# The left-over rows of a feature transform, stacked within SBUF into one operand a quarter

## The chip, the cores and the metric

The kernel runs on one core of one Trainium2 chip. The metric is the device time of one execution in microseconds. The kernel before took 689.68 us as the median of three runs (688.99 to 689.81).

## What is computed

The reference is a transformer layer with a spectral mixer ahead of a gated network, for 2048 tokens of 640 features in float32.

```python
def _A_ref(x, w_r, w_i):
    X = jnp.fft.rfft2(x, axes=(-2, -1)) * (w_r + 1j * w_i)
    return jnp.fft.irfft2(X, s=(S, D), axes=(-2, -1))
h = x + _A_ref(_layernorm(x), A_w_r, A_w_i)
n = _layernorm(h)
out = h + ((n @ w_gate) * (n @ w_up)) @ w_down        # F = 1728
```

The two-dimensional transform is made of matrix products with tables of cosines and sines: the tokens in two steps (16 residues times 128), and the features in one. A real transform of 640 features has 321 frequencies, and 322 columns are kept (NQ).

## The kernel before

All work is put in order by hand. The tokens lie as 16 tiles of 128 partitions. The stages follow one another on TensorE:

- **Front** (lines 144 to 369). Each tile is loaded, its moments are taken, even and odd parts of the features are folded, and `s1_mm` makes the first token step. The result is `s1` (four quarters of 128 feature rows, float32) and `rest`, the left-over rows: with 161 folded rows a quarter does not fit 128 partitions, so 33 + 31 + 2 x 32 rows lie together in one tile of 128 partitions. `rest_split` (line 271) splits them into a high and a low part, `s1r[:, 0]` and `s1r[:, 1]`, so that the fast float32r passes of TensorE keep the accuracy: high x high, high x low and low x high.
- **The group loop** (lines 499 to 537). There are 16 groups (NG) of two frequencies and their mirrors. `d_mm(g)` is the feature transform of a group: four float32 products for the quarters against `fmt`, and then six float32r products of 322 columns for the left-over rows against `frt`. `d_out(g)` copies the result to SBUF on ScalarE in four pieces. `s2_mm(g)` is the second token step, into the one buffer `u`. `filt(g)` multiplies by the complex filter on VectorE: three instructions that read `u` and one that adds. `is2_mm(g - 1)` is the first inverse step, and `is2_out(g - 1)` takes its result out: `high` and `end` on ScalarE, `low` on VectorE, then `main` on ScalarE.
- **The rest** (lines 551 on): the inverse feature step, the second layernorm, and the gated network over 14 chunks, written as Strassen products. `t34(0)` (line 703) makes one of the operands of those products, `t3`, once for each half of the tokens.

In one turn of the loop TensorE has in its order: `s2_mm(g)`, `d_mm(g + 2)`, `is2_mm(g - 1)`. All the loads of the loop are issued by one queue, SyncE's: `load_wm(g + 3)` (128 KB of matrices, `bits`, and 644 KB of filter, `wts`) and `load_wi(g + 2)` (128 KB, `bits`). Each has three buffers that are used in turn, so `wts` of group g + 3 waits until `filt(g)` has read its own. The queue works in order: what is behind a waiting issue waits too. Each issue also takes one of eight completion semaphores in turn, and waits until the transfer eight places ahead of it has landed.

Of the kernel before, what the change touches and what calls it, by code (L numbers as in the profile page):

```python
# [12 lines left out]
F32R = mybir.dt.float32r  # L13
AF = mybir.ActivationFunctionType
# [7 lines left out]
NC = 14  # L22
FW = (160, 193, 161, 161)
FOFF = (0, 160, 353, 514)
NR = 4
AHEAD = 5
FOLDS = {0: (1, 2), 1: (3,), 2: (4,), 7: (9,), 9: (11,)}
# [11 lines left out]
def f32(ap):  # L39
    return ap.bitcast(F32)  # L40
# [29 lines left out]
def tile_spectral_glu(ctx: ExitStack, tc: tile.TileContext, x, wf, wgu, wlast, wdown, wdlast,  # L70
# [53 lines left out]
    def home(tag, shape, name, dt=F32):  # L124
        return keep.tile(shape, dt, tag=tag, name=name)

    def cut(t, o, *shape):
        v = t[:, o:o + int(np.prod(shape))]
        names = [f"d{i}" for i in range(len(shape))]
        return v.rearrange(f"p ({' '.join(names)}) -> p {' '.join(names)}", **dict(zip(names[1:], shape[1:])))  # L130

    tab = home("stage", [P, 1448], "tab")
    fmt, imt, cit = cut(tab, 0, 675), cut(tab, 676, 4, 161), cut(tab, 1320, P)
    frt = home("dA", [P, 2, 2, NQ], "frt", F32R)
    s1 = home("big", [P, 4, NG, P], "s1")
    s1r = home("wA", [P, 2, NG, P], "s1r", F32R)
    rest = home("qr", [P, NG, P], "rest")
# [167 lines left out]
    odd(0, nc.gpsimd)  # L305
    for t in range(NT):
        if t == 1:
            nc.gpsimd.dma_start(frt, frem)
        if t >= 1:
            fs = even(t)  # L310
            if t + 1 < NT and t + 1 not in ASIDE:
                fs.insert(1, (0.4, lambda: odd(t + 1, nc.vector)))
            if t < AHEAD:
                fs.insert(1 + (t <= 2), (0.2, lambda: scale_c(t)))
            if t == 1:
                fs, (recip, w, *left) = fs[1:], dve[1][0]
                for f in (c1[4], fs[0][1], fs[1][1], recip, fs[2][1], w):
                    f()
                dve[2].insert(0, left)
            elif t == 2:  # L320
                (ww, r), = dve[2]
                for f in (fs[0][1], ww, tail[2].pop(), fs[1][1], r, fs[2][1], fs[3][1]):
                    f()
            else:
                weave(fs, dve[t], t in FOLDS)
            for f in tail[t]:
                f()
            if t < AHEAD - 1:
                s1_rest(t - 1)
                main = lambda: s1_main(t - 1, PS1[t - 1][0], 0, 4)  # L330
                for f in acts[t][:1] + post[t] + ([*acts[t][1:], main] if t < 2 else [main, *acts[t][1:]]):
                    f()
            else:
                s1_main(t - 1, PS1[t - 1][0], 0, 4)
                s1_rest(t - 1)
                for f in post[t]:
                    f()
                if t + 1 in SCALE_ON_ACT:
                    scale_c(t + 1)
                for f in acts[t]:  # L340
                    f()
        else:
            e0 = [f for _, f in even(0)]
            c0[0]()
            for f in (e0[0], c0[1], e0[1], c0[2], c0[3], e0[2], c0[4], *f1[:-1]):
                f()
        if t in FOLDS:
            nc.gpsimd.tensor_copy(small.tile([P, 1], F32, tag="hold", name="hold"), folded(t)[1][:, 383:384])
            for k in FOLDS[t]:
                odd(k, nc.gpsimd)  # L350
        if t >= 1:
            for f in stats[t]:
                f()
            if AHEAD <= t + 1 < NT and t + 1 not in SCALE_ON_ACT:
                scale_c(t + 1)
        else:
# [22 lines left out]
    def load_wi(g):  # L379
        WI[g] = wis[g % 3]  # L380
        nc.sync.dma_start(WI[g], mm[g, :, 1])
# [5 lines left out]
    def parts(ps, main, rest):  # L387
        for k, (b, o, w, l, r) in enumerate(main):
            mmx(ps[b][:, o:o + w], l, r, k < 2, False)
        for k, (b, l, r) in enumerate(rest):  # L390
            mmx(ps[b][:, 0:NQ], l, r, False, k >= len(rest) - 2)

    def d_mm(g):
        ps = PD[g] = bank("re"), bank("im")
        where = ((1, 0), (0, 0), (1, 160), (0, 160))
        main = [(b, o, FW[c], s1[:, c, g], fmt[:, FOFF[c]:FOFF[c] + FW[c]]) for c, (b, o) in enumerate(where)]
        parts(ps, main, [(b, s1r[:, k, g], frt[:, l, b]) for k, l in ((0, 0), (0, 1), (1, 0)) for b in range(2)])

    def d_out(g):
        ps = PD[g]  # L400
# [98 lines left out]
    for g in range(3):  # L499
        load_wm(g)  # L500
        load_wi(g)
    d_mm(0)
    d_out(0)
    d_mm(1)
    d_out(1)
    for g in range(NG - 1):
        s2_mm(g)
        if g + 2 < NG:
            d_mm(g + 2)
        if g + 3 == NG:  # L510
            xt = home("big", [P, 2, 5, 2, 512], "xt", F32R)
            irt = xt[:, 1].rearrange("p k l n -> p (k l n)")[:, 0:5 * NQ].rearrange("p (c q) -> p c q", c=5)
            nc.gpsimd.dma_start(irt, irem)
        if g == NG - 2:
            s2_mm(g + 1)
            filt_half(g, 0, True)
            is2_out(g - 2)
        if g >= 1:
            is2_mm(g - 1)
        if g < NG - 2:  # L520
            filt(g)
        else:
# [12 lines left out]
        if g == 6:  # L535
            nc.sync.dma_start(cit, ci)
            nc.sync.dma_start(imt, imain)
# [164 lines left out]

    def t34(m):
        src = TJ["b"][:, :, 2 * m:2 * m + 2].rearrange("p j k n -> p k j n")
        hi, lo = ((t3[:, :, l] if m == 0 else xt[:, 1, 0:2, l]).rearrange("p k (j n) -> p k j n", j=4)
                  for l in range(2))
        if m:
            return [lambda: act(hi, src, AF.Copy), lambda: tt(lo, src, f32(hi), op=OP.subtract)]

        def low():  # L710
            for k in range(2):
                nc.vector.scalar_tensor_tensor(lo[:, k], src[:, k], -1.0, f32(hi[:, k]), op0=OP.mult, op1=OP.subtract)

        return [lambda: act(hi, src, AF.Copy, scale=-1.0), low]

    def transp(t):
        turn_mm(t)
# [77 lines left out]
    for t in range(NT):  # L795
        for k in tside[t]:
            turn_mm(k)
        if t + 2 < NT:
            unfold(t + 2, dside[t], tside[t])
        else:  # L800
            for k in tside[t]:
                turn_hi(k)
                turn_lo(k)
        if t + 3 < NT:
            id_mm(t + 3)
        for f in aside[t]:
            f()
        if t == NT - 3:
            is1_mm(t)
            ht = home("qm", [P, 9216], "ht", F32R)  # L810
            hop, t3 = cut(ht, 0, 7, 2, 512), cut(ht, 7168, 2, 2, 512)
# [136 lines left out]
    def strassen(c, blk, ahead, downs, side):  # L948
# [46 lines left out]
        product(oa, False, ws, 640, [(t3[:, k, 0], t3[:, k, 1]) for k in range(2)])  # L995
        tt(c22, oa, c22, op=OP.add)
        tt(ob if odd else h1, ob, c22, op=OP.mult)  # L997
        if odd:
# [42 lines left out]
    for n, (blk, p) in enumerate(steps):  # L1041
        if p == 6:
# [28 lines left out]
            else:  # L1071
# [25 lines left out]
                    return pieces((t1s[:, 0, m, k], t1s[:, 1, m, k]), pb[k])  # L1097

                def t34(m, k):
                    return pieces((t3[:, k, 0], t3[:, k, 1]), pd[k], -1) if m == 0 else pieces(  # L1100
                        (xt[:, 1, k, 0], xt[:, 1, k, 1]), pb[k])

                hi(0, range(2))
# [148 lines left out]
def tables():  # L1252
# [19 lines left out]
    def rows(kind, ds):  # L1272
        r = np.zeros((len(ds), 2, NQ))
        for i, d in enumerate(ds):
# [3 lines left out]
            else:  # L1278
# [7 lines left out]
    frem = np.concatenate([rows("ee", np.arange(128, 161)), rows("oe", np.arange(1, 32)),  # L1286
                           np.stack([rows("os", np.arange(1, 33)), rows("eo", np.arange(32))], 1).reshape(64, 2, NQ)])

    m = np.zeros((32, 128, 128), np.float64)
    im = np.zeros((32, 128, 128), np.float64)  # L1290
    kidx = np.zeros((32, 64), np.int64)
# [46 lines left out]
    for b in range(2):  # L1338
# [1 line left out]
        irem[0:64, (2, 4)[b]] = rest[b, :, 1]  # L1340
    irem[0, 3] = irem[64, 3] = inv[0, 192, 0]

    return dict(cc=f4(fwd), ci=f4(fwd.T), fmain=f4(fmain), frem=split(frem), imain=f4(imain), irem=irem,
                mm=f4(mm)), fr, kidx


# [32 lines left out]
```

## Time and profile before

| What | Value |
|---|---|
| median of three runs | 689.68 us |
| the profiled execution's own time | 689.28 us |
| its span on the core | 687.5 us |
| TensorE busy in the span | 676.1 us (98%) |
| VectorE, ScalarE, GpSimd busy | 70%, 47%, 56% |
| group loop, first `s2_mm` to last | 42.63 to 106.40 us |
| granted TensorE clock | 1.0 in every slice |

The profile is of one execution, and 1.8 us of its time lie outside the span. The table's busy shares are means over stages with different limits. The group loop, which the change touches, is about a tenth of the span. Times in the views count from the span's start.

### The profile page before, as it was taken

What the parts mean: (1) busy time and instruction counts of PE and PEld (TensorE: products, weight loads), DVE (VectorE), ACT (ScalarE), POOL (GpSimd) and SP (SyncE); (2) the same over time, 40 slices, a digit from 0 to 9 for tenths busy, and PEclk for the clock granted to TensorE, in tenths of its full rate; (3) what the DMA queues carried; (4) which work ended last, traced back from release to release, by engine and by line L of the source; (5) the groups of instructions that cost most, each with busy time, mean ns of one, the idle gap of its engine ahead of it and who ended that gap; (6) DMA issues with size and microseconds to landing.
All of it is one profiled execution on the core that took longest, in us unless ns stands there. A gap on an engine that the chain in (4) does not pass through costs nothing.

```text
span 687.5 us, 10293 instructions
## 1 busy us (share of the span) xinstructions
PE 676.1 (98%) x3744; PEld 597.6 (87%) x3744; DVE 483.4 (70%) x985; ACT 322.3 (47%) x623; POOL 383.0 (56%) x364
## 2 busy tenths in 40 slices
PE   8999999999999999999999999999999999999998
PEld 8989998887788888888888889788888888888887
DVE  7968887897963968786776647753757575766654
ACT  6966665375543434262635236542525252525310
POOL 3101114331097987787887623286987878797610
PEclk9999999999999999999999999999999999999999
DMA  9516663000121212125243239301212120212003
GB/s 328 203 55 215 238 205 119 1 1 26 52 78 39 76 39 77 40 82 106 82 62 99 89 75 275 111 0 40 78 39 77 39 77 38 77 40 77 1 1 153
DMA packets 43602, 60.30 MB, mean 88 GB/s; under 512 B 23584, under 2 KB 28448, under 8 KB 43552
## 3 DMA queue, kind: packets, MB, share of 16 engines
q1 hardware_dynamic: 42832, 57.78, 26.0%
q0 software_dynamic: 288, 1.48, 0.6%
q8 instruction: 29, 0.48, 0.3%
q10 hardware_dynamic: 432, 0.39, 0.2%
q14 instruction: 21, 0.17, 0.1%
HBM read 51.78 MB, written 7.86 MB: 87 GB/s over the span
## 4 chain that ended last, share of the span: by engine, by line
PE 75%; DVE 11%; DMA 5%; ACT 4%; POOL 2%; issue 2%; SPq 1%; DVEq 0%; ACTq 0%
PE e L110 37%; PE d L110 22%; PE re L110 2%; PE im L110 2%; PE u L414 2%; DMA x<-in_x_dram 2%; PE im L456 2%; PE eo L110 2%; DMA raw<-in_wgu_dram 2%; PE im L242 1%; DMA z<-zfar 1%; POOL wst L837 1%; PE ir L456 1%; DVE ht L942 1%; PE y L110 1%
## 5 line engine op out<-in xcount | busy, mean ns | idle before, releaser
L110 PE MATMUL e<-xt,wst 128*128 128x512 f32 x864 | 213.4, 391 | 0.2 <-ACT c L986 0.2
L110 PEld LDWEIGHTS e<-xt,wst 128*128 128x128 f32 x864 | 159.8, 188 | 31.1 <-ACT c L986 0.4
L923 DVE TENSOR_TENSOR x<-d,x 128x320 f32<-128x320 f32 x280 | 123.4, 484 | 48.7 <-PE d L110 44.5
L110 PE MATMUL d<-wd,ht 128*128 128x320 f32 x832 | 143.0, 308 | 0.0
L110 PEld LDWEIGHTS d<-wd,ht 128*128 128x128 f32 x832 | 130.8, 188 | 7.3
L837 POOL TENSOR_TENSOR wst<-raw,wst 128x1024 fp32r<-128x1024 f32 x23 | 56.3, 2449 | 64.5 <-ACT wst L836 63.3
L110 PE MATMUL e<-t,wst 128*128 128x512 f32 x288 | 74.1, 392 | 0.6 <-ACT h L978 0.6
L110 PE MATMUL d<-wt,ht 128*128 128x320 f32 x360 | 69.6, 311 | 0.5 <-DVE x L923 0.5
L853 POOL TENSOR_TENSOR wst<-raw,wst 128x896 fp32r<-128x896 f32 (+1 forms) x46 | 65.0, 1437 | 6.8 <-ACT wst L848 6.8
L110 PEld LDWEIGHTS e<-t,wst 128*128 128x128 f32 x288 | 52.7, 188 | 10.8 <-ACT h L978 1.4
L110 PEld LDWEIGHTS d<-wt,ht 128*128 128x128 f32 x360 | 57.3, 188 | 3.5 <-issue 1.0
L993 DVE TENSOR_TENSOR e<-e,h 128x512 f32<-128x512 f32 x24 | 16.8, 700 | 45.0 <-PE e L110 35.6
L848 ACT ACTIVATE wst<-raw 128x896 fp32r<-128x896 f32 (+1 forms) x48 | 30.2, 676 | 35.9 <-POOL raw L842 35.1
L978 ACT ACTIVATE h<-e 128x512 f32<-128x512 f32 x24 | 14.3, 596 | 68.3 <-PE e L110 63.6
L939 ACT ACTIVATE ht<-e 128x512 fp32r<-128x512 f32 x44 | 26.3, 597 | 40.4 <-DVE e L997 17.5
L485 POOL CAST qr<-bits 1x128 fp32r<-1x128 f32 x15 | 4.2, 280 | 71.4 <-DVE qr L489 71.4
L110 PE MATMUL e<-xt,wdir 128*128 128x512 f32 x180 | 42.6, 394 | 0.9 <-DVE ht L792 0.9
L110 PEld LDWEIGHTS e<-xt,wdir 128*128 128x128 f32 x180 | 33.4, 188 | 9.0 <-DVE ht L792 1.2
L942 DVE TENSOR_TENSOR ht<-e,ht 128x512 fp32r<-128x512 f32 x54 | 37.0, 686 | 1.6 <-ACT ht L939 1.3
L898 DVE TENSOR_TENSOR x<-d,x 128x320 f32<-128x320 f32 x62 | 27.5, 485 | 14.2 <-PE d L110 14.0
L110 PE MATMUL e<-ht,wst 128*128 128x512 f32 x144 | 37.1, 392 | 0.0
L581 ACT ACTIVATE wd<-draw 128x320 fp32r<-128x320 f32 (+1 forms) x30 | 15.7, 558 | 42.6 <-POOL draw L590 42.3
(213 smaller groups left out, 1230.6 us busy)
## 6 DMA issues: line engine op xcount, KB each, us to landing
raw<-in_wgu_dram SPq DMA_DIRECT2D x24, 640.0 KB, 3.9
wts<-in_wf_dram SPq DMA_DIRECT2D x16, 644.0 KB, 3.9
draw<-in_wdown_dram SPq DMA_DIRECT2D x24, 320.0 KB, 4.3
x<-in_x_dram SPq DMA_DIRECT2D x15, 320.5 KB, 6.0
out_dram<-x SPq DMA_DIRECT2D x15, 320.0 KB, 3.2
bits<-in_mm_dram SPq DMA_DIRECT2D x32, 128.0 KB, 3.8
zfar<-zr SPq DMA_DIRECT2D x32, 80.0 KB, 2.3
raw<-in_wgu_dram SPq DMA_DIRECT2D x4, 320.0 KB, 4.1
```

Of the source, the lines that this page charges most:

```text
L110: nc.tensor.matmul(o, l, r, start=start, stop=stop, skip_group_check=True)
L456: nc.tensor.matmul(out, y[:, h, a:b], inv(g, h), start=n == 0, stop=n == len(ys) - 1)
L581: act(o[:, 0, a:a + n], src, AF.Copy)
L837: ptt(wa[:, 1], stage[:, 0:1024], f32(wa[:, 0]), op=OP.subtract)
L848: act(ws[:, 0, o:o + b - a], stage[:, a:b], AF.Copy)
L853: ptt(ws[:, 1, o:o + b - a], stage[:, a:b], f32(ws[:, 0, o:o + b - a]), op=OP.subtract)
L898: tt(xv, ps[b][:, 0:320], xv, op=OP.add)
L923: tt(xv, o, xv, op=OP.add)
L939: act(hop[:, a, 0], src, AF.Copy)
L942: engine.tensor_tensor(hop[:, a, 1], src, f32(hop[:, a, 0]), op=OP.subtract)
L978: act(h0, oa, AF.Copy)
L993: tt(ob, ob, h1, op=OP.add)
```

## The change

For groups 3 to 15 the six float32r products of `d_mm` become four, one for each quarter of the output columns. Before, every product had all 128 left-over rows against all 322 columns of one half of the output, though a quarter's rows meet only their own 160 to 194 columns. Now a quarter's rows are stacked three times, high, low and high, on 93, 99, 96 and 96 partitions, against a table with high, high and low rows. One product over the stack gives the same three terms. Groups 0 to 2 keep the six products (PLAIN).

The stacks are made by `stack(g, n)`: for n groups at a time it issues, on SyncE's queue, 12 transfers from SBUF to SBUF, three for each quarter, of 31, 33, 32 and 32 rows, each row n x 512 bytes. There are two buffers: `dC` for three groups and `qt` for two. The stacks for groups 3 to 5 and 6 to 7 are issued ahead of the loop, those for groups 8 to 10, 11 to 12 and 13 to 15 in turns 3, 5 and 8 of the loop, when the buffer's last reader is in TensorE's order.

Besides, the table `frt` grows from 1288 to 1966 columns (one load on GpSimd's queue in the front stage), and since `qt` takes 4 KB of each partition, the tile `ht` is shorter, and `t3` lies in two tiles. In `t34(0)` ScalarE writes it with two instructions of 512 columns in place of one of 1024.

```diff
+RROWS = ((33, 31, 1), (0, 33, 1), (64, 32, 2), (65, 32, 2))
+RW = (160, 194, 162, 162)
+PLAIN = 3
+AGAIN = {3: (8, 3), 5: (11, 2), 8: (13, 3)}
...
-    frt = home("dA", [P, 2, 2, NQ], "frt", F32R)
+    frall = home("dA", [P, 4 * NQ + sum(RW)], "frt", F32R)
+    frt = cut(frall, 0, 2, 2, NQ)
...
-        parts(ps, main, [(b, s1r[:, k, g], frt[:, l, b]) for k, l in ((0, 0), (0, 1), (1, 0)) for b in range(2)])
+        if g < PLAIN:
+            parts(ps, main, [(b, s1r[:, k, g], frt[:, l, b]) for k, l in ((0, 0), (0, 1), (1, 0)) for b in range(2)])
+            return
+        parts(ps, main, [])
+        for q, ((r, n, _), (b, o), w) in enumerate(zip(RROWS, RWHERE, RW)):
+            a = 4 * NQ + sum(RW[:q])
+            mmx(ps[b][:, o:o + w], ST[g][0:3 * n, q], frall[0:3 * n, a:a + w], False, q >= 2)
...
+    def stack(g, n):
+        o = home("dC" if n == 3 else "qt", [P, 4, n, P], "st", F32R)
+        for q, (r, m, s) in enumerate(RROWS):
+            for i, l in enumerate((0, 1, 0)):
+                nc.sync.dma_start(f32(o[i * m:i * m + m, q]),
+                                  f32(s1r[r:r + s * (m - 1) + 1:s, l, g:g + n]))
...
+    stack(3, 3)
+    stack(6, 2)
     d_mm(0)
...
         if g + 2 < NG:
             d_mm(g + 2)
+        if g in AGAIN:
+            stack(*AGAIN[g])
...
-        return [lambda: act(hi, src, AF.Copy, scale=-1.0), low]
+        def high():
+            for k in range(2):
+                act(his[k], src[:, k], AF.Copy, scale=-1.0)
```

TensorE's order in one group, before: `d_mm` has the four products with `tab` and six with `frt` and `s1r`, and the inverse step (`ir`, `im` from `y`) follows.

```order
L110 MATMUL re<-tab,s_88 128x161
L110 MATMUL re<-frt,s1r 128x322
L110 MATMUL im<-frt,s1r 128x322
L110 MATMUL re<-frt,s1r 128x322
L110 MATMUL im<-frt,s1r 128x322
L110 MATMUL re<-frt,s1r 128x322
L110 MATMUL im<-frt,s1r 128x322
L456 MATMUL ir_705<-bits,y 65x32x4 x2
```

The same place now; `st` is the stack.

```order
L115 MATMUL re<-tab,s_88 128x161
L115 MATMUL im<-frt,st 128x160
L115 MATMUL re<-frt,st 128x194
L115 MATMUL im<-frt,st 128x162
L115 MATMUL re<-frt,st 128x162
L479 MATMUL ir_781<-bits,y 65x32x4 x2
```

Six rows of 322 columns became four of 160 to 194, and the half `re`, which ScalarE reads first, is now finished by the last row and not by the last but one.

SyncE's queue from the last load ahead of the loop (`bits` of the inverse matrices of group 2), before, with the loads for groups 3, 4 and 5 behind it:

```order
L381 DMA bits<-in_mm_dram 128x256
L375 DMA bits<-in_mm_dram 128x256
L376 DMA wts<-in_wf_dram 128x1288
L375 DMA bits<-in_mm_dram 128x256
L376 DMA wts<-in_wf_dram 128x1288
L381 DMA bits<-in_mm_dram 128x256
L375 DMA bits<-in_mm_dram 128x256
```

The same place now, up to the stack of turn 3:

```order
L387 DMA bits<-in_mm_dram 128x256
L417 DMA st<-s1r 31x384 x3
L417 DMA st<-s1r 33x384 x3
L417 DMA st<-s1r 32x384 x6
L417 DMA st<-s1r 31x256 x3
L417 DMA st<-s1r 33x256 x3
L417 DMA st<-s1r 32x256 x6
L381 DMA bits<-in_mm_dram 128x256
L382 DMA wts<-in_wf_dram 128x1288
L381 DMA bits<-in_mm_dram 128x256
L382 DMA wts<-in_wf_dram 128x1288
L387 DMA bits<-in_mm_dram 128x256
```

Twenty-four transfers now stand ahead of the loads of group 3, and further down twelve stand ahead of the loads of groups 6, 8 and 11.

What the issues of the first stack wait for; `DMAHW0` to `DMAHW7` are the eight completion semaphores, ScalarE and VectorE the makers of `s1r`:

```order
L417 DMA st<-s1r 31x384 [waits DMAHW4_49,Activation_49]
L417 DMA st<-s1r 31x384 [waits DMAHW5_49,DVE_49]
L417 DMA st<-s1r 31x384 [waits DMAHW6_49]
L417 DMA st<-s1r 33x384 [waits DMAHW7_49]
L417 DMA st<-s1r 33x384 [waits DMAHW0_49]
L417 DMA st<-s1r 33x384 [waits DMAHW1_49]
L417 DMA st<-s1r 32x384 [waits DMAHW2_49]
L417 DMA st<-s1r 32x384 [waits DMAHW3_49]
L417 DMA st<-s1r 32x384 [waits DMAHW4_49]
L417 DMA st<-s1r 32x384 [waits DMAHW5_49]
L417 DMA st<-s1r 32x384 [waits DMAHW6_49]
L417 DMA st<-s1r 32x384 [waits DMAHW7_49]
```

The ninth transfer of a stack waits for the first to land, the tenth for the second, and so on.

More of the change, by code (lines that the diff above doesn't have):

```diff
@@ L24 @@
 FOFF = (0, 160, 353, 514)
+RROWS = ((33, 31, 1), (0, 33, 1), (64, 32, 2), (65, 32, 2))
+RWHERE = ((1, 0), (0, 0), (1, 160), (0, 160))
+RW = (160, 194, 162, 162)
+PLAIN = 3
+AGAIN = {3: (8, 3), 5: (11, 2), 8: (13, 3)}
 NR = 4
@@ L307, in tile_spectral_glu @@
         if t == 1:
-            nc.gpsimd.dma_start(frt, frem)
+            nc.gpsimd.dma_start(frall, frem)
         if t >= 1:
@@ L396, in d_mm @@
         main = [(b, o, FW[c], s1[:, c, g], fmt[:, FOFF[c]:FOFF[c] + FW[c]]) for c, (b, o) in enumerate(where)]
-        parts(ps, main, [(b, s1r[:, k, g], frt[:, l, b]) for k, l in ((0, 0), (0, 1), (1, 0)) for b in range(2)])
+        if g < PLAIN:
[5 more added lines that the diff above has]
+            mmx(ps[b][:, o:o + w], ST[g][0:3 * n, q], frall[0:3 * n, a:a + w], False, q >= 2)
+    ST = {}
+    def stack(g, n):
[4 more added lines that the diff above has]
+                                  f32(s1r[r:r + s * (m - 1) + 1:s, l, g:g + n]))
+        for i in range(n):
+            ST[g + i] = o[:, :, i]
     def d_out(g):
@@ L704, in t34 @@
         src = TJ["b"][:, :, 2 * m:2 * m + 2].rearrange("p j k n -> p k j n")
-        hi, lo = ((t3[:, :, l] if m == 0 else xt[:, 1, 0:2, l]).rearrange("p k (j n) -> p k j n", j=4)
-                  for l in range(2))
         if m:
+            hi, lo = (xt[:, 1, 0:2, l].rearrange("p k (j n) -> p k j n", j=4) for l in range(2))
             return [lambda: act(hi, src, AF.Copy), lambda: tt(lo, src, f32(hi), op=OP.subtract)]
+        his, los = ([t3[k][:, l].rearrange("p (j n) -> p j n", j=4) for k in range(2)] for l in range(2))
+        def high():
+            for k in range(2):
+                act(his[k], src[:, k], AF.Copy, scale=-1.0)
         def low():
             for k in range(2):
-                nc.vector.scalar_tensor_tensor(lo[:, k], src[:, k], -1.0, f32(hi[:, k]), op0=OP.mult, op1=OP.subtract)
-        return [lambda: act(hi, src, AF.Copy, scale=-1.0), low]
+                nc.vector.scalar_tensor_tensor(los[k], src[:, k], -1.0, f32(his[k]), op0=OP.mult, op1=OP.subtract)
+        return [high, low]
     def transp(t):
@@ L809, in tile_spectral_glu @@
             is1_mm(t)
-            ht = home("qm", [P, 9216], "ht", F32R)
-            hop, t3 = cut(ht, 0, 7, 2, 512), cut(ht, 7168, 2, 2, 512)
+            ht = home("qm", [P, 8192], "ht", F32R)
+            hop = cut(ht, 0, 7, 2, 512)
+            t3 = [cut(ht, 7168, 2, 512), home("qt", [P, 2, 512], "t3", F32R)]
             banks("a", "pglu")
@@ L994, in strassen @@
         at(4)
-        product(oa, False, ws, 640, [(t3[:, k, 0], t3[:, k, 1]) for k in range(2)])
+        product(oa, False, ws, 640, [(t3[k][:, 0], t3[k][:, 1]) for k in range(2)])
         tt(c22, oa, c22, op=OP.add)
@@ L1099, in t34 @@
                 def t34(m, k):
-                    return pieces((t3[:, k, 0], t3[:, k, 1]), pd[k], -1) if m == 0 else pieces(
+                    return pieces((t3[k][:, 0], t3[k][:, 1]), pd[k], -1) if m == 0 else pieces(
                         (xt[:, 1, k, 0], xt[:, 1, k, 1]), pb[k])
@@ L1287, in tables @@
                            np.stack([rows("os", np.arange(1, 33)), rows("eo", np.arange(32))], 1).reshape(64, 2, NQ)])
+    left = [rows(*a) for a in (("oe", np.arange(1, 32)), ("ee", np.arange(128, 161)), ("os", np.arange(1, 33)),
+                               ("eo", np.arange(32)))]
     m = np.zeros((32, 128, 128), np.float64)
@@ L1341, in tables @@
     irem[0, 3] = irem[64, 3] = inv[0, 192, 0]
-    return dict(cc=f4(fwd), ci=f4(fwd.T), fmain=f4(fmain), frem=split(frem), imain=f4(imain), irem=irem,
+    stacked = np.zeros((128, sum(RW)), np.float32)
+    for q, (t, (b, o), w) in enumerate(zip(left, RWHERE, RW)):
+        h, l = split(t[:, b, o:o + w]).transpose(1, 0, 2)
+        stacked[0:3 * len(h), sum(RW[:q]):sum(RW[:q + 1])] = np.concatenate([h, h, l])
+    frem = np.concatenate([split(frem).reshape(128, -1), stacked], 1)
+    return dict(cc=f4(fwd), ci=f4(fwd.T), fmain=f4(fmain), frem=frem, imain=f4(imain), irem=irem,
                 mm=f4(mm)), fr, kidx
```

## The prediction

> **What bounds the kernel now.** I read the page first, then the chain of waits over the group loop, then the timelines of ScalarE and VectorE there, then the transfers.
>
> The page's first row says that TensorE is busy nearly all the time:
>
> ```profile
> PE 676.1 (98%) x3744; PEld 597.6 (87%) x3744; DVE 483.4 (70%) x985; ACT 322.3 (47%) x623; POOL 383.0 (56%) x364
> ```
>
> A busy share of the whole span doesn't say what ends last in the loop. The chain of waits does. Its columns are start, length, and what; this is one turn of the loop:
>
> ```profile
> 55.93 1.09 PE u L414 x4
> 57.02 0.27 PE im L110 x2
> 57.29 0.33 PE re L110 x2
> 57.61 0.28 PE im L110 x2
> 57.89 0.42 PE re L110 x3
> ...
> 59.05 0.44 PE ir L456 x4
> 59.49 0.89 PE im L456 x8
> 60.38 1.09 PE u L414 x4
> ...
> 91.57 1.09 PE u L414 x4
> ...
> 104.94 0.54 PE re L414 x2
> ```
>
> There is no wait in it: TensorE sets the turn, 60.38 - 55.93 = 4.45 us. I call the start of `s2_mm(g)` S(g): S(3) is 55.93, S(4) 60.38, S(11) 91.57, S(14) 104.94. In a turn `s2_mm` takes 1.09, the four main products 1.15 (57.02 to 58.17), the left-over rows 0.88 (six passes of 0.147 up to 59.05), and `is2_mm` 1.33.
>
> The same turn on ScalarE (first two rows) and VectorE shows how near the next bound is:
>
> ```profile
> 54.55 0.43 ACT L402 ACTIVATE t<-re 64x322 f32<-64x322 f32 x1 [1.44 <-PE re L110]
> ...
> 56.73 0.27 ACT L471 ACTIVATE bits<-ir 1x128 f32<-1x128 f32 x1
> ```
>
> ```profile
> 57.03 0.42 DVE L489 TENSOR_TENSOR qr<-ir,qr 64x256 fp32r<-64x256 f32 x1 [0.68 <-PE u L414]
> 57.48 0.83 DVE L420 TENSOR_TENSOR y<-u,wts 128x644 f32<-128x644 f32 x1
> ...
> 59.16 0.82 DVE L422 TENSOR_TENSOR us<-u,wts 64x644 f32<-64x644 f32 x1
> ```
>
> `d_mm(4)` ends, ScalarE takes it out and then the inverse step's rows (until 57.00), only then VectorE runs `low` (57.03) and `filt(3)`, whose third instruction releases `u` at 59.98, and `s2_mm(4)` begins at 60.38. This loop spans two turns (from S(2), 8.90 us before) and has 0.2 to 0.4 us of slack in them.
>
> **The passes removed.** A pass of 322 columns takes 0.147 us. Passes of 160 to 194 columns scale to about 0.08; the shortest spacing in the turn is that of `is2_mm`, 0.89 / 8 = 0.11. I take 0.10, so four take 0.40 for 0.88: TensorE's turn would be 3.97. The loop over ScalarE and VectorE gives less: `re`, which ScalarE reads first, is now finished last, a pass (0.15) later, so that loop shortens by 0.48 - 0.15 = 0.33 and its slack in two turns, to about 8.45, or 4.23 a turn. What is late next is VectorE's `low`, behind ScalarE. Over 12 turns that is a gain of 12 x 0.22 = 2.7 us, if nothing else waits.
>
> **The transfers added.** There are 60, in five stacks of 12, all on SyncE's queue ahead of loads that the loop needs. What an issue costs, from four that stand directly behind one another:
>
> ```profile
> 73.82 0.38 SPq L381 DMA_DIRECT2D bits<-in_mm_dram  x1
> 74.26 0.42 SPq L536 DMA_DIRECT2D tab<-in_ci_dram  x1
> 74.73 0.42 SPq L537 DMA_DIRECT2D tab<-in_imain_dram  x1
> 75.25 0.38 SPq L375 DMA_DIRECT2D bits<-in_mm_dram  x1
> ```
>
> That is 0.44 to 0.52; I take 0.45. A small load (`bits`, 8 KB for each of 16 engines) lands after 2.0 us at best, as the answer on its line, 375, says (first row below), and the rate of the engines is read from three stretches (the last two columns are the share of the 16 engines' time and GB/s):
>
> ```profile
> DMA to landing us min/median/max: 2.0/3.4/7.9
> ```
>
> ```profile
> 51.00:68.00 17.00, 17.00 (x115) 15.66 (x114) 13.72 (x19) 11.05 (x27) 2.93 (x8) 1.00 0.63 213
> ```
>
> ```profile
> 52.00:54.00 2.00, 2.00 (x15) 1.83 (x14) 1.43 (x3) 1.08 (x3) 0.73 (x2) 1.00 0.91 346
> ...
> 423.00:428.00 5.00, 5.00 (x30) 4.55 (x29) 3.42 (x8) 3.63 (x6) 2.60 (x2) 1.00 1.03 408
> ```
>
> 346 / 0.91 / 16 = 23.8 GB/s for one engine; the loop's mean gives 213 / 0.63 / 16 = 21.1, the best stretch 408 / 16 = 25.5. A `bits` load spends 8 KB / 23.8 = 0.34 us of its 2.0 moving, so 1.66 us is fixed.
>
> The question on which all hangs is over how many engines a transfer of 31 rows is spread. No transfer in this trace has such a count. Those that it has are cut evenly: of 23,584 packets under 512 bytes, 32 x 640 are `zr`'s pieces of 128 bytes, and the other 3,104 are 16 for each of the 194 transfers (two rows of the list of them are shown), one from each engine.
>
> ```profile
> DMA packets 43602, 60.30 MB, mean 88 GB/s; under 512 B 23584, under 2 KB 28448, under 8 KB 43552
> ```
>
> ```profile
> zfar<-zr SPq DMA_DIRECT2D x32, 80.0 KB, 2.3
> ...
> tab<-in_ci_dram SPq DMA_DIRECT2D x1, 64.0 KB, 3.7
> ```
>
> All have a multiple of 16 rows. 32 rows can be cut so, 2 a piece; 33 only into 11 pieces of 3 (or 3 of 11); 31 is prime, so an even cut leaves all 31 rows to one engine. The price of such a transfer of three groups (47.6 KB) is between 0.13 us (16 engines) and 2.0 us (one, 23.8 GB/s). I take the even cut, as the rows have nothing else: 2.0 us, and 1.33 for two groups, one behind another on one engine, which also has its 16th of every other load (40 KB of `wts`, 1.7 us).
>
> The Trainium skill, "DMA: Bandwidth & Descriptors", section "Why a DMA increments its semaphore by 16 and not by 1", has this as a rule: a transfer uses the largest count up to 16 that divides the slowest dimension of both sides, so 31 rows take one engine and 33 take 11. No run here shows it yet. By it the sum below stands; against it, the first rival does.
>
> With eight semaphores the ninth transfer of a stack waits for the first to land, the eleventh for the third. So a stack holds the queue until its third 31-row transfer is in. Step by step:
>
> ```profile
> 39.07 2.28 ACT L272 ACTIVATE s1r<-rest 128x256 fp32r<-128x256 f32 x5
> ```
>
> *Ahead of the loop.* The high rows of groups 4 to 7 are there after the third of these five, at about 40.4. The three transfers land at 40.4 + 1.66 + 2.0 = 44.1, 46.1, 48.1; the eleventh is issued then, the second stack from 49.0, whose three land at 52.0, 53.3, 54.7. Its last is issued at 55.1, `bits` of group 3 at 55.6 (before: under 46), landed at 57.6. S(3) is 57.8 for 55.93: **+1.9**. `d_mm(3)` loses a little earlier (its last rows land at about 50.4), which this takes in.
>
> *Turn 3.* `d_mm(5)` ends at 57.8 + 2.6 = 60.4 and frees the buffer. The loads of groups 3 to 5, held back, now lie together on the slow engine (three `wts` and four `bits`, 6.5 us from about 57): the stack starts 1.9 late. The third lands at 60.4 + 1.66 + 6.0 + 1.9 = 70.0, `bits` of group 6 is issued 0.9 later and lands at 72.9. S(6) is 73.0 for 55.93 + 3 x 4.45 = 69.3: **+3.7** in all.
>
> *Turn 5.* Six loads are issued first, then the stack at 73.6, with 2.1 us of theirs still on the engine: third landed at 81.4, `bits` of group 8 at 84.3. S(8) is 84.4 for 78.2: **+6.2**.
>
> *Turn 8.* The buffer is free at 84.4 + 2.6 = 87.0; the engine is 3.3 us behind (three `wts`, six `bits` and two tables). Third landed at 98.2, `bits` of group 11 at 101.1. S(11) is 101.2 for 91.57: **+9.6**.
>
> *The end.* Three more turns of 4.23 give back 0.7: S(14) is **+8.9**. What follows the loop starts from its end, and so moves by as much.
>
> With 25.5 GB/s each engine time is 7% less, about 0.8 us for each of the four steps: +5.7. With 21.1 it is 13% more: +13.7.
>
> **The rest.** The larger `frt` load and the two instructions of `t34(0)`:
>
> ```profile
> frt<-in_frem_dram POOLq DMA_DIRECT2D x1, 644.0 KB, 6.9
> ```
>
> ```profile
> 9.00:12.00 3.00, 3.00 (x27) 2.84 (x26) 2.96 (x18) 2.16 (x8) 1.68 (x4) 1.00 1.04 390
> ```
>
> ```profile
> 187.00 1.06 ACT L714 ACTIVATE ht<-bt 128x1024 fp32r<-128x1024 f32 x1 [1.80 <-DVE bt L697]
> ...
> 191.13 0.59 ACT L978 ACTIVATE h<-e 128x512 f32<-128x512 f32 x1
> ```
>
> 339 KB more while the engines are full (390 GB/s) hold the last tiles back by 0.87 us at most; they are used 10 us later, so I take 0.2. Two of 0.59 for one of 1.06 add 0.12, on ScalarE's way to the network's first chunk. `t3` in two tiles costs nothing else.
>
> The sum, against the profiled execution's own 689.28 (0.4 under the median): 689.28 + 8.9 + 0.3 = **698.5**.
>
> **The rivals.**
>
> *The 31 rows are spread over all engines (686.9).* Then a transfer lands 1.8 us after its issue, no semaphore is waited for, a stack takes 12 x 0.45 = 5.4 us, and `bits` of group 6 lands 2.6 + 5.4 + 2.0 = 10 us after S(3), ahead of its use at 12.7. The gain of 2.7 stays: 689.28 - 2.7 + 0.3. It decides wherever three transfers take under about 4 us together. For it: nothing but that the case isn't in the trace.
>
> *One engine, but faster by itself (692).* All rates above are of 16 engines that share the memory's side; alone, and within SBUF, one may do more than 25.5. At 28 the same steps give about +2.5. For it: packets in the two fast stretches come from memory; against it: their shares of 0.91 and 1.03 are the engines' own.
>
> *The clock falls in the waits (702.5).* TensorE would stand still for some 3 us ahead of S(8) and 4 ahead of S(11). If that lowers its clock, one turn's 3.97 us taken at half speed costs 4 more. In this trace the granted clock is 1.00 in each stretch above, and the chain has no wait in the loop to show it. The Trainium skill, "TensorE: Matmul & The Clock Gate", Part 1, says that an idle stretch of about 3.4 us halves the clock until TensorE has been busy for as long. By that it would be half of 3.4, 1.7 us, for a wait of that length.
>
> **How the numbers follow.** Forecast 0.63, spread 0.13, faster engine 0.15, clock 0.09. A measurement of this kernel can tell about 0.2% (1.4 us) from no change: the spread case is faster, a third of the faster engine's falls within 0.2%, the rest is slower: 0.14, 0.06, 0.80. The range runs from 689 (most of the faster engine's case) to 705 (the slow bound, 703.3, and the clock); it leaves out the spread case and a few above.
>
> **What would show it.** Right: small packets grow by 132 for a stack (3 x 1 + 3 x 11 + 6 x 16), not by 192; `st` transfers of 31 rows land after 4 to 8 us, three in steps of 2; waits of TensorE at `s2_mm` of groups 3, 6, 8 and 11 behind `bits` loads; S(14) near 113.8. Wrong: `st` landing in about 2 us and turns of 4.2 without waits (the first rival), turns under 4.1 (then the loop over ScalarE isn't the next bound), or waits at `filt` for `wts` in place of `s2_mm`.

## The result, and the profile after

| | before | after |
|---|---|---|
| median | 689.61 us | 709.54 us |
| lowest to highest (4 runs each) | 688.99 to 689.81 | 708.10 to 711.33 |
| the profiled execution's own time | 689.28 us | 708.10 us |

The ratio is 1.029, with a 95% interval of 1.026 to 1.032. The change made the kernel 19.9 us slower. 698.5 was forecast, with a range from 689 to 705, and the measurement lies outside it. The side was right, and the size was a little under half of what came.

From the page of the changed kernel: TensorE's share, and the packets.

```profile
PE 678.6 (96%) x3718; PEld 597.8 (85%) x3718; DVE 485.0 (69%) x985; ACT 322.7 (46%) x624; POOL 383.4 (54%) x364
...
DMA packets 46183, 63.22 MB, mean 90 GB/s; under 512 B 24244, under 2 KB 31028, under 8 KB 46132
```

TensorE's share fell from 98 to 96%. The packets under 512 bytes grew by 24,244 - 23,584 = 660 = 5 x 132. That is the count that the prediction named for one engine for a 31-row transfer and 11 for a 33-row one.

TensorE's timeline in the loop, its waits at `s2_mm` of groups 3, 6, 8 and 11 (start, length; in brackets the idle time before, and what ended it):

```profile
60.49 2.48 PE L437 MATMUL u<-t,bits 128*128 128x322 f32 x4 [3.53 <-DMA bits<-in_mm_dram]
...
78.07 1.32 PE L437 MATMUL u<-t,bits 128*128 128x322 f32 x4 [2.21 <-DMA bits<-in_mm_dram]
...
91.48 2.48 PE L437 MATMUL u<-t,bits 128*128 128x322 f32 x4 [3.68 <-DMA bits<-in_mm_dram]
...
110.29 2.04 PE L437 MATMUL u<-t,bits 128*128 128x322 f32 x4 [3.43 <-DMA bits<-in_mm_dram]
```

The four waits stand where they were forecast, behind the load that was forecast. Three of the four `s2_mm` behind them take 2.0 to 2.5 us in place of about 1.1 to 1.3. The windows say why; the third column from the right is the granted clock:

```profile
59.55:66.38 6.83, 5.89 (x19) 5.12 (x20) 3.05 (x4) 0.28 (x1) 0.00 (x0) 0.50 0.99 332
90.27:97.10 6.83, 5.62 (x18) 4.85 (x19) 2.98 (x4) 0.01 (x1) 0.09 (x1) 0.50 0.98 310
110.75:114.17 3.42, 3.42 (x12) 2.82 (x11) 1.34 (x2) 0.00 (x0) 0.00 (x0) 0.50 1.01 327
```

5.89 + 5.62 + 3.42 = 14.9 us of work were done at half speed, which is 7.5 us more than at full speed.

SyncE's queue, the stacks and the loads of `bits` behind them (24 issues are the first two stacks):

```profile
40.25 17.70 SPq L417 DMA_DIRECT2D st<-s1r  x24
58.06 0.53 SPq L381 DMA_DIRECT2D bits<-in_mm_dram  x1
...
66.07 9.53 SPq L417 DMA_DIRECT2D st<-s1r  x12
75.64 0.59 SPq L381 DMA_DIRECT2D bits<-in_mm_dram  x1
...
97.02 10.56 SPq L417 DMA_DIRECT2D st<-s1r  x12
107.62 0.59 SPq L381 DMA_DIRECT2D bits<-in_mm_dram  x1
```

And the chain of waits, through the first two stacks and at the loop's end:

```profile
41.76 6.94 DMA st<-s1r
48.72 0.46 SPq L417
...
57.36 0.59 SPq L417
57.95 0.06 issue
58.06 2.29 DMA bits<-in_mm_dram
...
124.73 0.54 PE re L437 x2
```

The third 31-row transfer lands at 48.7 (48.1 was forecast) and the queue goes on. From there to the load of `bits` the chain has no landing in it: the second stack (49.86 to 57.95) is twelve issues, one directly behind another, of 0.51 to 0.79 us, 0.68 from one to the next in the mean. 0.45 was taken for one.

S(14) moved from 104.94 to 124.73, by 19.8. On TensorE this is made up of 14.9 us of added waits (the four above, 1.03 in `d_mm(3)`, and 1.05 at `s2_mm(7)`), 7.5 of half clock, and 2.6 that the shorter turns give back (what is left of the sum).

### The profile page after: what moved, and what is told of

Its sections match the earlier page's. It is cut to its first block, busy times and chain, and to the rows that moved or that the text cites. A ratio compares the mean times of both kernels' runs of the same rounds, so it can differ in the third digit from the quotient of the medians.

```text
span 706.3 us, 10324 instructions
## 1 busy us (share of the span) xinstructions
PE 678.6 (96%) x3718; PEld 597.8 (85%) x3718; DVE 485.0 (69%) x985; ACT 322.7 (46%) x624; POOL 383.4 (54%) x364
## 2 busy tenths in 40 slices
DMA packets 46183, 63.22 MB, mean 90 GB/s; under 512 B 24244, under 2 KB 31028, under 8 KB 46132
## 4 chain that ended last, share of the span: by engine, by line
PE 73%; DVE 10%; DMA 7%; SPq 3%; ACT 3%; issue 2%; POOL 1%; ACTq 0%; DVEq 0%
PE e L115 40%; PE d L115 24%; DMA st<-s1r 4%; SPq L417 2%; DMA x<-in_x_dram 2%; PE eo L115 2%; PE u L437 1%; PE im L248 1%; DMA bits<-in_mm_dram 1%; DVE ht L974 1%; PE re L115 1%; PE y L115 1%; PE im L115 1%; DMA raw<-in_wgu_dram 1%; POOL wst L869 1%
## 5 line engine op out<-in xcount | busy, mean ns | idle before, releaser
L955 DVE TENSOR_TENSOR x<-d,x 128x320 f32<-128x320 f32 x280 | 123.2, 483 | 48.7 <-PE d L115 44.6
L115 PE MATMUL e<-t,wst 128*128 128x512 f32 x360 | 94.5, 392 | 0.3 <-ACT h L1010 0.3
L115 PEld LDWEIGHTS e<-t,wst 128*128 128x128 f32 x360 | 66.2, 188 | 13.6 <-ACT h L1010 1.0
L437 PE MATMUL u<-t,bits 128*128 128x322 f32 x56 | 21.3, 509 | 15.3 <-DMA bits<-in_mm_dram 12.9
```

What stands on the lines that cost most here:

```text
L115: nc.tensor.matmul(o, l, r, start=start, stop=stop, skip_group_check=True)
L437: nc.tensor.matmul(ps[h][:, 0:NQ], WM[g][0][:, h], T[g][:, h], start=True, stop=True)
L955: tt(xv, o, xv, op=OP.add)
```

## The experiments

All kernels are edits of the changed kernel.

**The queue.** Are the loads late because they stand behind the transfers, or because the transfers take the engines?

```
-                nc.sync.dma_start(f32(o[i * m:i * m + m, q]),
+                nc.gpsimd.dma_start(f32(o[i * m:i * m + m, q]),
```

> The same 60 transfers, issued on GpSimd's queue in place of SyncE's. Queue theory (what costs is that the loads of the loop stand behind the transfers on one queue): the loads leave as before the change, no wait for `bits` is left, TensorE's clock stays at 1.0, and the time is 686 to 688 us (689.6 less 2.7 for the shorter turns, plus 0.3). Landing theory (what costs is that a 31-row transfer sits on one engine for 2 us and that the loads share this engine): the waits stay, at the stacks or at the loads, and the time is above 700.

Measured: 689.87 (interval of the ratio 0.9999 to 1.0017), no change from before, and over the queue theory's range. No wait for `bits` is left, and all but 3 of the 22.8 us between the changed kernel and its passes alone (below) are gone. They weren't all lost to the place in the queue, because this edit does two things: on GpSimd's queue a 31-row transfer doesn't sit on one engine. One of three groups lands after 1.9 us in the median, where one engine needs 2.0 us for moving it alone, and the seventh experiment has the count of packets. So this run by itself doesn't refute the landing theory; the third experiment, which leaves the transfers on SyncE's queue, separates the two. But 3.1 us are missing against the passes alone. The profiled run, which took 691.63, has lost as much in the loop (S(14) at 105.23, in the passes alone 102.14), at one place. TensorE's timeline, and the window behind it:

```profile
51.19 0.31 PE L115 MATMUL re<-frt,st 96*128 96x162 f32 x1 [1.85 <-DMA st<-s1r]
```

```profile
52.55:55.97 3.42, 3.42 (x11) 2.61 (x10) 1.22 (x2) 1.99 (x5) 2.09 (x5) 0.50 0.54 193
```

The first stack's last rows are late for `d_mm(3)` by 1.85 us, and half clock follows for 3.42, which costs 1.7. Not every run has that stretch: three of eleven (691.3 to 691.7 us) have a mean granted clock of 0.998, which is what one such stretch makes of 690 us, and the other eight, at 0.999 to 1.0, took 688.7 to 690.3. So the median holds the wait without the half clock, and about 1.2 us of its 3.1 have no cause shown.

**The clock.** TensorE is kept at work in three of the four waits.

```
+        if g in (3, 8, 11):
+            for _ in range(12):
+                nc.tensor.matmul(ps[0][:, 0:P], fmt[:, 0:P], fmt[:, P:2 * P], start=True, stop=True)
         for h in range(2):
```

> The changed kernel with 12 products of 128 columns that nothing reads ahead of `s2_mm` of groups 3, 8 and 11, into the buffer that `s2_mm` then overwrites, so that TensorE works in most of those three waits (about 2.6 of 3.5 us each). Clock theory: the granted clock stays at 1.0, the 7.7 us that the three half-speed stretches take (half of the 5.9, 5.6 and 3.9 us of work in them) are gone, and the time is 701 to 703. Rival (the loads arrive when they arrive, and TensorE only waits longer where it works faster): less than 2 us are gained, 707 to 710.

Measured: 708.29, a gain of 1.3, less than the changed kernel's own runs lie apart: the clock theory's size falls. In the profiled run the clock did stay at 1.0 behind those three waits (its mean is 0.998, in the three other runs 0.990 to 0.997, and all four took 707.7 to 708.7). But the wait at `s2_mm(6)` grew, and now it was this one that brought half clock:

```profile
77.97 2.48 PE L440 MATMUL u<-t,bits 128*128 128x322 f32 x4 [4.17 <-DMA bits<-in_mm_dram]
```

S(6) is 77.97 with the full clock and 78.07 without. The stack of turn 3 was issued from 63.26 on and not from 66.07, but its last issues stood until the 31-row transfers had landed. SyncE's queue, the ninth, tenth and eleventh issue of this stack:

```profile
70.22 0.48 SPq L417 DMA_DIRECT2D st<-s1r  x1
72.23 0.46 SPq L417 DMA_DIRECT2D st<-s1r  x1
74.24 0.46 SPq L417 DMA_DIRECT2D st<-s1r  x1
```

Steps of 2.01 us, the 2.0 that the prediction worked out for 47.6 KB on one engine. The eleventh issue, which waits for the third 31-row transfer, comes at nearly the same time in all three stacks of the loop, here and in the changed kernel: 74.24 and 74.50, 87.09 and 87.81, 106.02 and 106.48. So there are two chains here that end at nearly the same time, one over TensorE at half clock and one over the slow engine. Taking away the one bares the other.

**The 31 rows.** An even count, for 16 engines; the added row meets zeros in the table.

```
-RROWS = ((33, 31, 1), (0, 33, 1), (64, 32, 2), (65, 32, 2))
+RROWS = ((32, 32, 1), (0, 33, 1), (64, 32, 2), (65, 32, 2))
...
+    left[0] = np.concatenate([0 * left[0][:1], left[0]])
```

> The 31-row transfers take 32 rows (one more row of `s1r`, against a row of zeros in the table), so that all but the 33-row ones can be cut into 16. One-engine theory (the prediction's: a stack holds the queue until its third 31-row transfer is in): the waits within the stacks (1.4, 0, 1.8, 2.5 and about 2 us) are gone, and with them 6 to 8 us and one or two half-speed stretches, 697 to 702. Issue theory (the queue is held by the issues themselves, 0.6 to 0.8 us each, 8.1 a stack, whatever the rows): little is gained, 705 to 709.

Measured: 704.58, 5.0 us less than the changed kernel. It lies between the two theories, next to the issue theory's 705 to 709. The packets under 512 bytes are 24,469, which is 225 = 15 x (16 - 1) more: fifteen transfers went from one engine to 16. The waits within the first three stacks are all but gone (0.8 us in the first two together, 0.2 in the third), and the stacks are still long (the first two):

```profile
40.15 16.95 SPq L417 DMA_DIRECT2D st<-s1r  x24
57.21 0.53 SPq L381 DMA_DIRECT2D bits<-in_mm_dram  x1
```

So the one engine is worth 5 of the 20 us. 24 issues take 17 us without it, and that alone keeps `bits` of group 3 late. The stacks of turns 5 and 8 take 10.1 and 9.9 us, since issues wait there for loads that went out ahead of the stack: the seventh of turn 5 stands until a `wts` load issued at 74.76 has landed at 82.14, eight places ahead of it. The clock does not decide here either: of the four runs the one with a mean granted clock of 0.990 took 704.50, and the one with 0.998 took 704.66.

**The passes alone.** No transfers; `still` is a tile of zeros.

```
-    stack(3, 3)
-    stack(6, 2)
...
+    for g in range(PLAIN, NG):
+        ST[g] = still[:, :, g % 3]
...
-        if g in AGAIN:
-            stack(*AGAIN[g])
```

> The four passes a group alone: the stacks hold zeros set once ahead of the loop, and no transfer is issued, so the left-over rows of groups 3 to 15 are left out of the result. The prediction's gain of 2.7 us: 686 to 688 us and turns of 4.2 us. Rival (the loop over ScalarE and VectorE gives nothing back): turns of 4.45 and 689 to 690. Rival (the loop gives more than the sum says): turns under 4.1 and under 685.5.

Measured: 686.77 (ratio 0.9948 to 0.9976), 2.8 us under before. The chain, groups 4 and 6:

```profile
59.45 1.30 PE u L437 x4
...
67.99 1.29 PE u L437 x4
```

8.54 us for two turns, 4.27 a turn; 4.23 was forecast.

**The first stack's time.** GpSimd's queue again, with a turn more for the first stack.

```
-PLAIN = 3
-AGAIN = {3: (8, 3), 5: (11, 2), 8: (13, 3)}
+PLAIN = 4
+AGAIN = {4: (9, 3), 6: (12, 2), 9: (14, 2)}
...
```

> The transfers on GpSimd's queue as in the first experiment, and four groups with six passes in place of three, so that the first stack (groups 4 to 6) has one turn more to land. First-stack theory (GpSimd's queue lost 3.1 us against the kernel with no transfer at all, and all of it at the first stack: 1.85 us of waiting in `d_mm(3)` and 3.4 us at half clock right behind): no wait and no half-speed stretch in the loop, and 12 x 0.23 = 2.8 less 0.2 for the fourth group: 686.9 to 687.3 us. Rival (the transfers cost the loop something in every turn): 688.5 or more.

Measured: 687.88 (0.9965 to 0.9984). There is no wait for `st` and no half clock in the loop; the time is 0.6 over the expected range and 0.6 under the rival's. So the first stack explains 2.0 of the 3.1 us. In the profiled run S(14) is 2.2 us under before, close to the 2.4 expected from 2.8 less 0.2 and a start of the loop that lies 0.2 later in this run; where the rest of the time goes behind the loop stays open.

**Another order on the same queue.** With the same groups on SyncE, later stacks go out three to six transfers a turn, behind that turn's loads.

```
+    EACH = (3, 3, 3, 3, 6, 6, 4, 4, 4, 6, 6, 0, 0, 0, 0)
...
+        for _ in range(EACH[g]):
+            later.popleft()()
```

> All transfers on SyncE's queue as in the changed kernel, with four groups of six passes as in the fifth experiment, but the second and later stacks are issued three to six transfers a turn, behind that turn's loads, and not twelve together ahead of them. Order theory (the loss comes from the loads standing behind twelve transfers at once; the queue has the time for all, 4 x 0.65 + 3 x 0.47 = 4.0 us of a turn of 4.23): TensorE doesn't wait for `bits`, 687 to 689 us. Amount theory (60 issues and 15 one-engine transfers are too much for this queue, wherever they stand): waits of TensorE at `s2_mm` stay, 692 us or more.

Measured: 703.1. My order theory is refuted: `bits` is hardly late any more, but now the transfers are. Two of TensorE's waits (the longest of all, in a later group, is 4.56 us), and SyncE's queue ahead of the first:

```profile
70.11 0.31 PE L116 MATMUL re<-frt,st 96*128 96x162 f32 x1 [3.08 <-DMA st<-s1r]
...
82.72 0.31 PE L116 MATMUL im<-frt,st 96*128 96x162 f32 x1 [2.76 <-DMA st<-s1r]
```

```profile
54.78 2.46 SPq L567 DMA_DIRECT2D st<-s1r  x3
58.21 0.34 SPq L382 DMA_DIRECT2D bits<-in_mm_dram  x1
59.70 0.33 SPq L383 DMA_DIRECT2D wts<-in_wf_dram  x1
60.12 0.38 SPq L388 DMA_DIRECT2D bits<-in_mm_dram  x1
61.58 1.79 SPq L567 DMA_DIRECT2D st<-s1r  x3
```

The queue's time isn't all its own. From 57.24 to 61.58 it issued three loads in 1.05 us and stood for the other 3.3. The three longest waits in it, 0.9, 1.1 and 1.1 us, are for the landing of earlier transfers of `st` and of a `wts` load; the transfers behind stood too. My 4.0 us a turn had left that out. The amount theory's number (692 or more) came, but not by its waits.

**Issue against transport.** The third experiment with 512 bytes a row.

```
-                nc.sync.dma_start(f32(o[i * m:i * m + m, q]),
-                                  f32(s1r[r:r + s * (m - 1) + 1:s, l, g:g + n]))
+                nc.sync.dma_start(f32(o[i * m:i * m + m, q, 0:1]),
+                                  f32(s1r[r:r + s * (m - 1) + 1:s, l, g:g + 1]))
...
-            ST[g + i] = o[:, :, i]
+            ST[g + i] = o[:, :, 0]
```

> The third experiment (no 31-row transfer) with each transfer cut to the rows of one group, 512 bytes a row in place of 1536 or 1024, so that two or one of every three groups read rows that are not theirs and their left-over rows are wrong. The number of issues is kept, the bytes are 16 of 41. Issue theory (what is left in the third experiment is the time that SyncE's queue takes to issue twelve, 8.1 us, whatever they carry): within 2 us of its 704.6. Transport theory (the loads are late because the engines are busy with the rows): under 698.

Measured: 701.44 (699.3 to 705.9 in 4 runs), 3.1 under the third experiment: 1.1 outside the issue theory's 2 us, and 3.4 above the transport theory's 698. Neither range was met; the issue theory's is the nearer. The queue, and the landing:

```profile
39.88 16.32 SPq L417 DMA_DIRECT2D st<-s1r  x24
```

```profile
st<-s1r SPq DMA_DIRECT2D x45, 16.0 KB, 2.0
```

Transfers of 16 KB that land in 2.0 us hold the queue nearly as long (16.3) as those of 48 and 32 KB (16.9). So ahead of the loop what is left of the loss is issuing. In the loop it is not all: the stack of turn 5 takes 10.15 us here too, and as in the third experiment its seventh issue waits for a `wts` load (issued at 74.04, landed at 81.42).

**Half of them.** Only the six 32-row transfers of a stack.

```
-        for q, (r, m, s) in enumerate(RROWS):
+        for q, (r, m, s) in list(enumerate(RROWS))[2:]:
...
```

> The changed kernel with half of its transfers: only the 32-row ones (the third and fourth quarter) are issued, six a stack, and the passes of the first two quarters read those rows too, so that their left-over rows are wrong. A stack takes 6 x 0.6 = 3.8 us of the queue; the two ahead of the loop end at about 48, and `bits` of group 3 lands 5 us ahead of its use. Queue theory: nearly the whole gain comes out, 686.5 to 688.5. Rival (any transfers in this place cost in proportion, half of the 22.8 us between 686.8 and 709.5): 695 to 700.

Measured: 687.12 (0.9949 to 0.9977), the whole gain.

```profile
40.20 7.59 SPq L417 DMA_DIRECT2D st<-s1r  x12
```

On SyncE's queue, twelve issues of 0.63 us end at 47.8, early enough for `bits` of group 3. The 31-row transfers are among those left out, so the time to set this against is the third experiment's 704.58. Against that too the loss isn't in proportion; it is a matter of whether a stack is through before its loads are due.

**32 rows on GpSimd's queue.** The fifth experiment with the third's edit, meant to price the one engine by itself.

> The fifth experiment with the 31-row transfers made 32 rows, as in the third. If a transfer on one engine only costs where something stands behind it in a queue, this is the fifth's time within 0.4 us; if the one engine, which has its share of every load too, holds the loads back by itself, this is faster by over 0.5 us.

Measured: 687.91 against 687.88, no difference. But there was no one engine to take away. The packets of the fifth experiment, and of this one:

```profile
DMA packets 45522, 63.01 MB, mean 92 GB/s; under 512 B 24619, under 2 KB 29498, under 8 KB 45472
```

```profile
DMA packets 45522, 63.03 MB, mean 92 GB/s; under 512 B 24619, under 2 KB 29483, under 8 KB 45472
```

With 31 rows and with 32 the small packets are 24,619, where 15 transfers made 225 of difference on SyncE's queue. So on GpSimd's queue the 31 rows are spread already, and what one engine costs with nothing due behind it isn't shown. What the run does give is the price of the queue with the rows alike: the third experiment has the same 32 rows on SyncE's queue and takes 704.58, 16.7 us more, of which some 2.0 are the first stack's extra turn (the first experiment against the fifth).

**A better version.** All transfers, on two queues.

```
-                nc.sync.dma_start(f32(o[i * m:i * m + m, q]),
+                (nc.gpsimd if q < 2 else nc.sync).dma_start(f32(o[i * m:i * m + m, q]),
```

> The changed kernel, complete, with its transfers on two queues: the 31- and 33-row ones on GpSimd's, the 32-row ones on SyncE's, and three groups of six passes as in the change. Each queue has six a stack, which SyncE's carried without loss in the ninth experiment, and the first stack is issued in 3.8 us in place of 6.2 (GpSimd's alone) or 9.6. Queue theory: no wait for `bits`, `d_mm(3)` waits for its rows by under 0.5 us, and the time is 686.8 to 687.6, 0.3 to 0.4% under the kernel before. Rival (the 31-row transfers, one behind another on one engine, are late for `d_mm(3)` whatever queue issues them, and half clock follows the wait): 688.5 to 690.

Measured: 687.33, ratio 0.9961 (0.9948 to 0.9975): 2.0 us under the kernel before, and 22 under the changed one. The 31-row transfers are now on the queue that spreads them, so the place in the queue and the one engine are both taken away here. The chain runs through TensorE, with the turns of the kernel without transfers:

```profile
59.23 1.18 PE u L437 x4
...
67.75 1.19 PE u L437 x4
```

## Why the prediction was half right

*The gain: right, in part by luck.* 2.7 were forecast, the passes alone gave 2.8, with turns of 4.27 for 4.23. The 12 turns from S(2) to S(14) gave 2.3 of it, and 0.5 came ahead of S(2), which was not in the sum. Nor do 8.45 us for two turns follow from the rows: 8.90 less 0.33 and less a slack of 0.2 to 0.4 are 8.2 to 8.4. The larger table and the two instructions of `t34(0)` were put at 0.3; in the fourth experiment S(0) didn't move (42.62 for 42.63), and 0.1 were lost at the network's first chunk.

*One engine for 31 rows: right on SyncE's queue, and not the largest part.* The packets say it twice (660, and 225 without it), and the steps of 2.01 us. This is the rule of the Trainium skill, "DMA: Bandwidth & Descriptors", "Why a DMA increments its semaphore by 16 and not by 1"; the trace agrees. But taken away it gave 5 us of 20.

*"I take 0.45" for an issue: the step that failed.* An issue of a copy within SBUF takes 0.63 us of this queue with 32 rows and 0.80 with 33, so a stack costs 8.1 us by itself, not 5.4. The row that I took it from was of loads from memory. With 8.1 the question "on which all hangs", one engine or 16, isn't the one that decides: two stacks ahead of the loop take 16 us either way, and the first rival's 686.9, which rested on 5.4, couldn't have come. With the 31 rows spread on this queue, the third experiment took 704.58.

*The clock as a rival by itself: wrongly put, and worth little by itself.* Step by step against the forecast, with the times that the rows give:

| step | forecast | measured | with the clock held (second experiment) | where the added difference of "measured" lies on its chain |
|---|---|---|---|---|
| S(3) | 57.8 | 60.49 | 60.28 | the two stacks end 2.5 later, landing 0.2 |
| S(6) | 73.0 | 78.07 | 77.97 | half clock from S(3) to the next stack's start, 5.6 us for 2.6; stack 9.6 for 10.5; landing 0.3 |
| S(8) | 84.4 | 91.48 | 90.91 | stack 10.3 for 8.7; landing 0.4 |
| S(11) | 101.2 | 110.29 | 109.64 | half clock, 5.5 for 2.6; stack 10.6 for 12.1; landing 0.6 |
| S(14) | 113.8 | 124.73 | 123.25 | half clock, 1.7 |

Of the 10.9 us between forecast and measurement, 3.0 + 2.9 + 1.7 = 7.6 lie at half clock on this chain; the queue's part is 2.5 - 0.9 + 1.6 - 1.5 = 1.7, and the landings' 1.5. I had foreseen waits of 3 and 4 us, and gave the clock's fall in them a chance of 0.09 and a price of 4. It comes with them. But where a time lies on the chain isn't yet what it costs. In the second experiment the clock is full from S(3) to the next stack and from S(8) to the next, and S(3) to S(6) takes 17.69 us for 17.58, S(8) to S(11) 18.73 for 18.81: the stack starts earlier and stands longer, until the slow engine is through. S(14) comes 1.5 us earlier, and is still 9.4 over the forecast.

So these 9.4 us are the forecast's error without the clock. (The one stretch at half clock that is left, behind S(6), isn't on the chain there: the stack of turn 5 follows the queue's loads at 78.44.) 2.5 of them are the two stacks ahead of the loop, and 0.8 the two issues behind the third landing of each stack in the loop (1.16 us for 0.9): both are the price of an issue. 2.4 are the slow engine: the third landing came 11.0, 8.6 and 11.4 us after the first issue of the stack, not 9.6, 7.8 and 11.2. The rest are slower landings of `bits` and longer turns between. None of them alone makes the 9.4.

*Two slips in the sums.* Turn 8's terms add up to 98.0 and not 98.2. And if 7% of engine time are 0.8 us a step, 13% are 1.5, which puts the slow bound at 704.5 and not 703.3. The first would take 0.2 from the forecast; the second leaves the bound within the range.

*The first rival's question was put wrongly too.* "It decides wherever three transfers take under about 4 us together": in the third and eighth experiment transfers land in 1.9 to 2.3 us (the medians of those whose landing the trace has), and the time is 704.6 and 701.4.

## What to carry to other kernels

Count what a queue has to issue before a load that is due, in issues and not in bytes, and take the price from an issue of the same kind; where no row shows that kind, the bound has to be wide. On SyncE's queue a transfer whose count of rows has no divisor near 16 is a transfer on few engines, and whatever waits for a semaphore behind it waits for that. Before a cost on the chain is called the cause, take it away: half clock was 7.6 us of the chain here, and holding the clock gave 1.3. Before work is put on the queue that feeds the loop, look for one that stands idle: the same 60 transfers cost 22.8 us where they stood (709.5 against 686.8 without them), 3.1 on GpSimd's queue, and 0.6 on two queues. GpSimd's queue also spreads the 31 rows, and the issues take GpSimd's own time (414.1 us busy with all 60, 383.4 with none).

## What the runs showed of the hardware

*The price of an issue.* SyncE's queue took 0.47 us from issue to issue for loads of 128 rows from memory, 0.63 for copies within SBUF of 32 rows (with 512, 1024 and 1536 bytes a row alike), and 0.80 for 33 rows. GpSimd's took 0.51 for each of these copies. Why 33 rows cost more than 32, and a copy more than a load, wasn't tried. The Trainium skill, "DMA: Bandwidth & Descriptors", "Issuing engines are not separate DMA queues", says that issuing on several engines only saves the time of issuing, "which is usually small relative to the DMA itself". Here it is the larger part: 8.1 us for a stack of three groups, whose 384 rows of 1536 bytes (590 KB) would take 1.55 us of 16 engines at the prediction's 23.8 GB/s each (an estimate).

*When the clock falls.* Half clock came in stretches of 3.41 us or twice that, and what preceded it was not a wait of a certain length. Stretches of 3.41 us, in step with the changes of the clock, of the changed kernel (first two fences), of the first and of the third experiment; the third figure is TensorE's busy time:

```profile
56.14:59.55 3.41, 0.81 (x8) 0.62 (x6) 2.22 (x4) 2.56 (x7) 0.73 (x2) 1.00 0.24 62
59.55:62.96 3.41, 2.47 (x5) 1.71 (x6) 0.00 (x0) 0.00 (x0) 0.00 (x0) 0.50 1.03 302
62.96:66.38 3.42, 3.42 (x16) 3.42 (x15) 3.05 (x4) 0.28 (x1) 0.00 (x0) 0.50 0.95 361
```

```profile
76.61:80.02 3.41, 1.95 (x10) 1.66 (x11) 0.44 (x2) 1.05 (x3) 0.73 (x2) 1.00 0.86 262
```

```profile
49.14:52.55 3.41, 1.56 (x14) 1.43 (x14) 2.10 (x3) 0.99 (x3) 2.40 (x6) 1.00 0.96 276
```

```profile
101.54:104.95 3.41, 1.00 (x9) 0.81 (x8) 2.02 (x3) 2.74 (x7) 0.58 (x2) 1.00 0.49 123
```

Behind stretches with 0.81, 1.56 and 1.00 us of work the clock was halved; behind one with 1.95 (the wait of 2.21 us at `s2_mm(6)`, which lies across two stretches) it was not. It stayed at half behind 2.47 us of work and came back behind 3.42. So a wait of 1.85 us cost a stretch at half clock where one of 2.21 didn't. The prediction had cited the Trainium skill, "TensorE: Matmul & The Clock Gate", Part 1, for an idle stretch of about 3.4 us; the same part says that the window is free-running, and these rows agree with that. They don't agree with 3.4 us of idleness as the condition: 1.85 was enough. They agree with a limit between 1.56 and 1.95 us of work in a stretch, and a stretch of the third experiment narrows it: 1.72 us of work from 53.75 to 57.17 kept the clock at 1.0.
